# Attention with a feed-forward network on one core: the third step of pairs 2 and 3 computes block product 4 where the next pair's first FFN group stood, and the FFN groups move behind it

## The chip, the cores and the metric

The kernel runs on one core of one Trainium2 chip. The metric is the device time of one execution in microseconds. Ratios are worked out from the mean times of the fast runs of both kernels in the same rounds on the same chip, so they are not quite the ratio of the medians, nor always that of the plain means, that are quoted beside them. The span of a profiled execution is about 1.8 us shorter than its device time.

## The reference

Attention with a window of 96 keys and 8 global keys over 4 batches, 8 heads, 768 positions and a head size of 64. Its output, laid out as 3072 tokens of 512 values, goes through a feed-forward network (FFN) with a hidden size of 2048.

```python
scores = q @ k.T / sqrt(64) + bias         # kept: 8 global keys and the last 96 keys
a = softmax(where(keep, scores, -1e9))
x = (a @ v).transpose(0, 2, 1, 3).reshape(3072, 512)
r = maximum(x @ w_in, 0.0)                 # 512 -> 2048
out = (s * r * r + b) @ w_out              # 2048 -> 512
```

## The kernel before

The tokens are cut into 12 granules of 256. A step does the attention of two head pairs of one granule (two attention blocks, `stage_A`), computes the scores of the following step ahead of time, and has three slots, `c0`, `c1` and `c2`, for other work: the first goes before the first attention block, the second between the two blocks, the third after the second. A granule takes two steps.

In the second step of granule j its normalized attention output `xn` is transposed into `xT` by two DMA transposes in the SP queue. `u1(j, q)` is one FFN group of granule j: 16 matmuls that read `xT[j]` and `w_in` for a quarter of the hidden size, then a relu on ScalarE.

```python
    def finish_granule(j):
        ...
            x_by_dma(j)                      # xT[j] <- xn[j], two DMA transposes in the SP queue
        if 6 <= j + LEAD < NJ:
            hold_loads(xT[j][0:1, 0, GT - 1 : GT])   # loads of granule j+4 wait for xT[j]
            load_granule(j + LEAD)                   # six loads in the POOL queue: k, q, v, k, q, v

    def step(s, c0, c1, c2, pool=None, pre=()):
        ...
        if not last and j >= 4 and j + 2 < NJ:
            qk_by_dma(j + 2)                 # four DMA transposes in the SP queue
        posts = scores(s + 1)                # matmuls of the next step's scores
        ...
        run(exps); run(pre); run(masks)
        run(c0)
        stage_A(2 * s)                       # first attention block; normalized on VectorE
        flush()
        ...
        run(c1)
        stage_A(2 * s + 1, pool)             # second attention block, same PSUM buffer
        flush()
        ...
        run(c2[0:n])
        if last:
            finish_granule(j)
            if SHIFT < j + 2 < NJ:
                load_voff(j + 2)             # two more loads in the SP queue
        run(c2[n:])
        flush()
```

The second FFN matmul of two granules (a pair: granules 2*pr and 2*pr+1) is done as a 2x2 block product with seven block products in place of eight. `product(pr, n)` is one of them, 16 matmuls; `pe(pr, n)` is the product with its eviction queued for the next `flush`; `evac` reads its PSUM buffer on VectorE or ScalarE; `g_sum` and `weight_sums` make the sums of blocks that the products need, on VectorE; `join` adds partial results. Product 4 needs the last weight sum, `t4`. Products, FFN groups and some transposes share three PSUM buffers (`ps_h`); the attention blocks of these steps share one (`ps_av`).

Pairs 2, 3 and 4 run in this loop; pair pr starts at step 4*pr + 5. Its third step (`k0 + 2`, step 15 for pair 2) begins the FFN of granule 6, the next pair's first.

```python
    for pr in range(2, NJ // 2):
        ...
        step(
            k0 + 1,
            [u1(o, 2)],
            [u1(o, 3), g_sum(pr, 1, 0)],
            [g_sum(pr, 1, 1), pe(pr, 7), g_sum(pr, 2)],
            pre=[g_sum(pr, 3, 1)],
        )
        tail = k0 + 3 >= NU // 2
        step(
            k0 + 2,
            [u1(e + 2, 0), pe(pr, 5)] if tail else [pe(pr, 5), flush, pe(pr, 6)],
            [pe(pr, 6), g_sum(pr, 4, 0)] if tail else [g_sum(pr, 4, 0), u1(e + 2, 0)],
            [g_sum(pr, 4, 1), u1(e + 2, 1), join(pr, 1)] + [weight_sums[3]] * (pr == 2),
        )
        if tail:
            break
        step(
            k0 + 3,
            [pe(pr, 4)],
            [join(pr, 2), u1(e + 2, 2)],
            [u1(e + 2, 3)],
            pre=[join(pr, 0), pe(pr, 3), flush],
        )
```

The softmax here doesn't subtract the row's maximum and nothing guards it: scores larger than these inputs give would overflow.

Of the kernel before, what the change touches and what calls it, by code (L numbers as in the profile page):

```python
# [17 lines left out]
def kernel(  # L18
# [694 lines left out]
    def moe_p2_cols(j, tb, parts):  # L713
# [35 lines left out]
    weight_sums = [  # L749
        lambda: nc.vector.tensor_tensor(t1, w12, w11, ALU.subtract),  # L750
        lambda: nc.vector.tensor_tensor(t2, w22, t1, ALU.subtract),  # L751
        lambda: nc.vector.tensor_tensor(t3, w22, w12, ALU.subtract),
        lambda: nc.vector.tensor_tensor(t4, w21, t2, ALU.subtract),
    ]
# [3 lines left out]
    def quarter(j, half, c=None):  # L758
        lo, n = (0, NH) if c is None else (c * NH // 2, NH // 2)
        return g_of(j)[:, half * NH + lo : half * NH + lo + n, :]  # L760

    def g_sum(pr, n, c=None):

        def go():
            if pr not in gs_cur:
                gs_cur[pr] = [
                    gpool.tile([P, NH, GT], BF16, name="gsum", tag=f"gsum{i}", bufs=1)
                    for i in range(4)
                ]
            e, o = 2 * pr, 2 * pr + 1  # L770
            cs = slice(0, NH) if c is None else slice(c * NH // 2, (c + 1) * NH // 2)
            s1, s2, s3, s4 = (t[:, cs, :] for t in gs_cur[pr])
            dst, x, y, op = {
                1: (s1, quarter(o, 0, c), quarter(o, 1, c), ALU.add),
                2: (s2, s1, quarter(e, 0, c), ALU.subtract),
                3: (s3, quarter(e, 0, c), quarter(o, 0, c), ALU.subtract),
                4: (s4, quarter(e, 1, c), s2, ALU.subtract),
            }[n]
            nc.vector.tensor_tensor(dst, x, y, op)  # L779

        return go

    def unit_p1(j, q):

        for fp in (2 * q, 2 * q + 1):
            relu, _ = p1_mm(j, fp)
            relu()
        gs = g_of(j)[:, 4 * q : 4 * q + 4, :]
        if j % 2 or q == 3:
            outs.append(lambda: nc.vector.tensor_tensor(gs, gs, gs, ALU.mult))  # L790
        else:
            nc.scalar.activation(gs, gs, ACT.Square)
# [4 lines left out]
    def product(pr, n, tbs=range(GB), ps=None, cols=None):  # L797

        j = 2 * pr
        stat = {  # L800
            1: lambda: quarter(j, 0),
            2: lambda: quarter(j, 1),
            3: lambda: gs_cur[pr][3],
            4: lambda: quarter(j + 1, 1),
            5: lambda: gs_cur[pr][0],
            6: lambda: gs_cur[pr][1],
            7: lambda: gs_cur[pr][2],
        }[n]()
        mov = {1: w11, 2: w21, 3: w22, 4: t4, 5: t1, 6: t2, 7: t3}[n]
        cs = slice(0, CH) if cols is None else cols  # L810
        if ps is None:
            ps = ps_h.tile([P, GB, CH], F32, name="ps_2", tag="psh")
        prod_ps[pr, n] = ps
        for tb in tbs:
            for fc in range(NH):
                nc.tensor.matmul(  # L816
                    ps[:, tb, cs],
                    lhsT=stat[:, fc, tb * P : (tb + 1) * P],
                    rhs=mov[:, fc, cs],
                    start=(fc == 0),  # L820
                    stop=(fc == NH - 1),
                )

    def scaled(dst, ps, add):
        nc.vector.scalar_tensor_tensor(
            out=dst, in0=ps, scalar=s_bc[:], in1=add, op0=ALU.mult, op1=ALU.add
        )
# [6 lines left out]
    def both_blocks(ap):  # L834
        return ap.unsqueeze(1).to_broadcast((P, GB, CH))

    def put(pr, row, col, o, tb=None, c0=0, eng=nc.sync):

        b, g = divmod(2 * pr + row, NGR)
        t0 = b * S + g * GT  # L840
        cs = slice(col * CH, (col + 1) * CH)
        if tb is not None:
            t0 += tb * P
            c0 += col * CH
            eng.dma_start(out[t0 : t0 + P, c0 : c0 + o.shape[-1]], o)
        else:
            nc.sync.dma_start(out[t0 : t0 + GT, cs].rearrange("(a p) c -> p a c", p=P), o)
# [3 lines left out]
    def out_tile():  # L851

        n_out[0] += 1
        tag, bufs = (("first", 4), ("o_sb", 3))[n_out[0] % 2]
        return work.tile([P, GB, CH], F32, name="o_q", tag=tag, bufs=bufs)

    def store(pr, row, col, ps, add):

        o = out_tile()
        scaled(o[:].rearrange("p a c -> p (a c)"), ps, add)  # L860
        put(pr, row, col, o[:])

    def add_f32(dst, x, y):
        nc.vector.tensor_tensor(dst, x, y, ALU.add)

    def evac(pr, n):

        ps3 = prod_ps[pr, n][:]
        ps = ps3.rearrange("p a c -> p (a c)")
        if n == 1:  # L870
            res[pr] = [
                work.tile([P, GB, CH], F32, name=f"part{i}", tag=f"part{i}", bufs=1)
                for i in range(3)
            ]
            res[pr].append(out_tile() if pr == NJ // 2 - 1 else res[pr][0])
        r0, r1, r7, r6 = (t[:].rearrange("p a c -> p (a c)") for t in res[pr])
        if n == 1:
            scaled(res[pr][0][:], ps3, both_blocks(bvec[:, 0:CH]))
        elif n == 2:
            store(pr, 0, 0, ps, r0)  # L880
        elif n == 5:
            scaled(res[pr][1][:], ps3, both_blocks(bdiff[:]))
        elif n == 6:
            scaled(r6, ps, r0)
        elif n == 7:
            nc.scalar.activation(r7, ps, ACT.Copy, scale=s_bc[:])
        elif n == 3:
            store(pr, 0, 1, ps, r1)
        elif n == 4:
            store(pr, 1, 0, ps, r6)  # L890

    def join(pr, n):

        def go():
            _, r1, r7, r6 = (t[:].rearrange("p a c -> p (a c)") for t in res[pr])
            if n == 1:
                add_f32(r1, r1, r6)
            elif n == 0:
                add_f32(r6, r6, r7)
            else:  # L900
                o = out_tile()
                add_f32(o[:].rearrange("p a c -> p (a c)"), r7, r1)
                put(pr, 1, 1, o[:])

        return go

    def pe(pr, n):

        def go():
            product(pr, n)  # L910
            outs.append(lambda: evac(pr, n))

        return go

    def u1(j, q):
        return lambda: unit_p1(j, q)

# [214 lines left out]
    def rest(j, tb):  # L1132
# [6 lines left out]
    step(  # L1139
        11,  # L1140
        [lambda: p2_mm(3, 1, 0, FC // 2), u1(4, 0)],
        [u1(4, 1)],
        late[2:4] + [shifted_copy, weight_sums[0]],
    )
    step(12, [lambda: rest(3, 1), u1(4, 2)], [weight_sums[1], u1(4, 3)], [weight_sums[2]])
    for pr in range(2, NJ // 2):
        e, o = 2 * pr, 2 * pr + 1
        k0 = 2 * e + 5
        if k0 >= NU // 2:
            break  # L1150
        step(
            k0,
            [pe(pr, 2)],
            [u1(o, 0)],
            [u1(o, 1), flush, g_sum(pr, 3, 0)],
            pre=[pe(pr, 1), flush],
        )
        step(
            k0 + 1,
            [u1(o, 2)],  # L1160
            [u1(o, 3), g_sum(pr, 1, 0)],
            [g_sum(pr, 1, 1), pe(pr, 7), g_sum(pr, 2)],
            pre=[g_sum(pr, 3, 1)],
        )
        tail = k0 + 3 >= NU // 2
        step(
            k0 + 2,
            [u1(e + 2, 0), pe(pr, 5)] if tail else [pe(pr, 5), flush, pe(pr, 6)],
            [pe(pr, 6), g_sum(pr, 4, 0)] if tail else [g_sum(pr, 4, 0), u1(e + 2, 0)],
            [g_sum(pr, 4, 1), u1(e + 2, 1), join(pr, 1)] + [weight_sums[3]] * (pr == 2),  # L1170
        )
        if tail:
            break
        step(
            k0 + 3,
            [pe(pr, 4)],
            [join(pr, 2), u1(e + 2, 2)],
            [u1(e + 2, 3)],
            pre=[join(pr, 0), pe(pr, 3), flush],
        )  # L1180
    join(pr, 0)()
    for n in (3, 4):
# [4 lines left out]
    e, o = 2 * pr, 2 * pr + 1  # L1187
# [50 lines left out]
```

## Time and profile before

| | before |
|---|---|
| median of 3 runs | 210.3 us (210.06 to 210.32) |
| profiled execution | 210.51 us, span 208.7 us |
| PE busy | 201.1 us, 96% of the span |
| VectorE, ScalarE busy | 160.0 us (77%), 128.6 us (62%) |

The page of the kernel before, first the span and the busy time of each engine, then the granted clock in 40 slices (9 stands for nine tenths of full speed or more; the mean of this run was 1.000), then the shares of the chain that ended last:

```profile
span 208.7 us, 5315 instructions
...
PE 201.1 (96%) x2183; PEld 160.0 (77%) x2191; DVE 160.0 (77%) x336; ACT 128.6 (62%) x200; POOL 68.9 (33%) x89
...
PEclk9999999999999999999999999999999999999999
...
PE 76%; DMA 9%; POOL 4%; SPq 4%; DVE 3%; issue 1%; POOLq 0%
```

TensorE is the bound. The busy times of three stretches of the kernel before (columns: stretch in us and its length, then for each engine busy us and instructions, the clock, the DMA share and GB/s) show where it is not busy late in the kernel:

```profile
...
113.40:114.60 1.20, 0.07 (x3) 0.06 (x2) 1.09 (x3) 0.00 (x0) 0.04 (x1) 1.00 1.51 122
114.60:130.00 15.40, 15.40 (x176) 13.43 (x177) 10.50 (x20) 10.73 (x15) 8.51 (x12) 1.00 1.52 140
130.00:182.00 52.00, 51.98 (x597) 45.07 (x596) 40.28 (x79) 31.23 (x45) 2.31 (x3) 1.00 0.65 92
```

The PE timeline of the kernel before in step 15 (columns: start us, length us, engine, line, operation, out<-in, shape, count, and in brackets the idle time before it and what ended it). The lines left out are the attention matmuls:

```profile
109.41 3.78 PE L816 MATMUL ps<-wsub,gsum 128*128 128x256 bf16 x32
...
114.57 1.91 PE L616 MATMUL ps<-xT,w_in_bf 128*128 128x256 bf16 x16 [1.13 <-DMA xT<-xn]
...
116.56 1.91 PE L616 MATMUL ps<-xT,w_in_bf 128*128 128x256 bf16 x16
118.40 0.62 PE L438 MATMUL ps_s<-qx,kx 64*128 64x128 bf16 x16
118.95 1.92 PE L816 MATMUL ps<-w_out_bf,gsum 128*128 128x256 bf16 x16
```

Products 5 and 6 start at 109.41. The first FFN group of granule 6 waits 1.13 us for the transposed activations. Where nothing waits, the next matmuls start 1.75 us after the start of a group that is listed as 1.91 us long: the listed times overlap by 0.16 us. The page "Perfetto Trace Analysis" of the Trainium skill (summary of the profiler window per engine type) calls the TensorE end estimated, and this trace agrees in so far as the listed end is not when the next matmul can start.

The SP queue of the kernel before, which issued those transposes (the length is that of issuing, not of the transfer):

```profile
101.31 0.53 SPq L684 DMA_DIRECT2D out_dram<-o_sb  x1
101.94 0.44 SPq L847 DMA_DIRECT2D out_dram<-o_q  x1
102.54 3.46 SPq L596 DMA_TRANSPOSE xT<-xn  x2
106.12 0.93 SPq L313 DMA_DIRECT2D vo<-vb  x1
```

The last line of the view of line 596, all transposes of activations in the kernel before:

```profile
DMA to landing us min/median/max: 2.4/4.3/9.9
```

The maximum, 9.9 us, is the transpose of granule 6 (the same view cut to 101 to 108 us gives 9.9 alone). A load that waits for the same landing shows when it came; the POOL timeline of the kernel before:

```profile
114.56 0.18 POOL L122 COPY gate<-xT 1x1 bf16<-1x1 bf16 x1 [12.69 <-DMA xT<-xn]
```

VectorE in the same step of the kernel before. The lines are, in order: the sum for product 6, the masks of the next step, the eviction of product 5, the reciprocal and the normalizing of the first attention block, then the reciprocal of the second, and the weight sum t4 in its old place:

```profile
109.94 1.23 DVE L779 TENSOR_TENSOR gsum<-gsum,gT 128x2048 bf16<-128x2048 bf16 x1
111.08 1.28 DVE L454 TENSOR_TENSOR pt<-pt,tmpl 128x1024 bf16<-128x1024 bf16 x2
112.29 0.74 DVE L825 SCALAR_TENSOR_TENSOR part<-ps,s_bc,bdiff 128x512 f32<-128x512 f32 x1
113.48 0.18 DVE L462 RECIPROCAL rc<-ps_av 128x4 f32<-128x4 f32 x1 [0.45 <-PE ps_av L492]
113.69 0.42 DVE L463 TENSOR_TENSOR xn<-ps_av,rc 128x256 bf16<-128x256 f32 x1
...
116.75 0.18 DVE L462 RECIPROCAL rc<-ps_av 128x4 f32<-128x4 f32 x1 [1.38 <-PE ps_av L492]
...
118.52 1.22 DVE L753 TENSOR_TENSOR wsub<-w_out_bf,wsub 128x2048 bf16<-128x2048 bf16 x1
```

### The profile page before, as it was taken

What the parts mean: (1) busy time and instruction counts of PE and PEld (TensorE: products, weight loads), DVE (VectorE), ACT (ScalarE), POOL (GpSimd) and SP (SyncE); (2) the same over time, 40 slices, a digit from 0 to 9 for tenths busy, and PEclk for the clock granted to TensorE, in tenths of its full rate; (3) what the DMA queues carried; (4) which work ended last, traced back from release to release, by engine and by line L of the source; (5) the groups of instructions that cost most, each with busy time, mean ns of one, the idle gap of its engine ahead of it and who ended that gap; (6) DMA issues with size and microseconds to landing.
All of it is one profiled execution on the core that took longest, in us unless ns stands there. A gap on an engine that the chain in (4) does not pass through costs nothing.

```text
span 208.7 us, 5315 instructions
## 1 busy us (share of the span) xinstructions
PE 201.1 (96%) x2183; PEld 160.0 (77%) x2191; DVE 160.0 (77%) x336; ACT 128.6 (62%) x200; POOL 68.9 (33%) x89
## 2 busy tenths in 40 slices
PE   6899999999999999999997999999999999999993
PEld 2677884557867585878886898888898889888883
DVE  7685689995989866799799784599785696737974
ACT  4975669485975558685763766564966665476200
POOL 8984334999646102705500906300000000000000
PEclk9999999999999999999999999999999999999999
DMA  5999999999999999999999999999451210240006
GB/s 167 170 181 206 207 207 172 155 152 135 115 147 143 155 157 193 120 265 188 145 207 128 113 133 174 184 208 100 52 158 49 77 28 0 50 154 0 0 4 200
DMA packets 110308, 28.17 MB, mean 135 GB/s; under 512 B 97836, under 2 KB 108780, under 8 KB 110284
## 3 DMA queue, kind: packets, MB, share of 16 engines
q0 software_dynamic: 75472, 13.11, 86.7%
q1 hardware_dynamic: 33612, 14.13, 39.0%
q10 hardware_dynamic: 1200, 0.59, 1.1%
q8 instruction: 17, 0.28, 0.6%
q14 instruction: 7, 0.06, 0.1%
HBM read 27.26 MB, written 6.29 MB: 161 GB/s over the span
## 4 chain that ended last, share of the span: by engine, by line
PE 76%; DMA 9%; POOL 4%; SPq 4%; DVE 3%; issue 1%; POOLq 0%
PE ps L616 35%; PE ps L816 19%; PE ps L664 13%; DMA xT<-xn 5%; DMA w_in_bf<-in_moe_w_in_dram 5%; PE ps_s L438 4%; PE ps_av L492 4%; SPq L357 3%; POOL nat L102 2%; POOL vb L108 2%; SPq L596 1%; PE ps_t L348 1%; POOL w_in_bf L140 1%; DVE o_early L697 1%; DVE wsub L751 1%
## 5 line engine op out<-in xcount | busy, mean ns | idle before, releaser
L616 PE MATMUL ps<-xT,w_in_bf 128*128 128x256 bf16 x768 | 90.5, 273 | 1.7 <-DMA xT<-xn 1.1
L626 ACT ACTIVATE gT<-ps 128x512 bf16<-128x512 f32 x96 | 55.7, 598 | 48.4 <-PE ps L616 48.2
L616 PEld LDWEIGHTS <-w_in_bf 128*128 128x128 bf16 x768 | 72.8, 98 | 11.3 <-issue 1.2
L447 ACT ACTIVATE pt<-ps_s 128x1024 bf16<-128x1024 f32 (+1 forms) x44 | 39.3, 946 | 3.2 <-PE ps_s L438 3.2
L664 PE MATMUL ps<-w_out_bf,gT 128*128 128x512 bf16 x120 | 28.9, 379 | 0.5 <-issue 0.2
L816 PEld LDWEIGHTS <-gsum 128*128 128x128 bf16 x256 | 24.1, 98 | 3.7 <-DVE gsum L779 0.5
L454 DVE TENSOR_TENSOR pt<-pt,tmpl 128x1024 bf16<-128x1024 bf16 (+1 forms) x40 | 24.5, 644 | 1.7 <-ACT pt L447 1.6
L790 DVE TENSOR_TENSOR gT<-gT 128x1024 bf16<-128x1024 bf16 x20 | 13.7, 685 | 11.6 <-ACT gT L626 11.6
L664 PEld LDWEIGHTS <-gT 128*128 128x128 bf16 x128 | 11.7, 98 | 13.2 <-issue 0.3
L463 DVE TENSOR_TENSOR xn<-ps_av,rc 128x256 bf16<-128x256 f32 x48 | 20.4, 424 | 1.7
L116 POOL DMA_DIRECT2D nat<-in_k_dram x20 | 17.7, 886 | 8.6 <-DMA w_in_bf<-in_moe_w_in_dram 2.1
L816 PEld LDWEIGHTS <-gT 128*128 128x128 bf16 x200 | 18.7, 98 | 2.3
L117 POOL DMA_DIRECT2D vb<-in_v_dram x20 | 18.4, 919 | 5.9 <-DMA nat<-in_k_dram 2.4
L116 POOL DMA_DIRECT2D nat<-in_q_dram x20 | 17.9, 896 | 6.9 <-DMA w_out_bf<-in_moe_w_out_dram 2.9
L462 DVE RECIPROCAL rc<-ps_av 128x4 f32<-128x4 f32 x48 | 8.6, 178 | 12.8 <-PE ps_av L492 10.6
L492 PEld LDWEIGHTS <-pt 128*128 128x128 bf16 x320 | 14.4, 98 | 2.7 <-DVE xn L463 0.7
L629 DVE TENSOR_TENSOR gT<-gT 128x512 bf16<-128x512 bf16 x32 | 13.0, 420 | 3.7 <-ACT gT L626 3.3
L492 PE MATMUL ps_av<-vb,pt 128*128 128x65 bf16 x208 | 15.4, 193 | 0.0
L816 PE MATMUL ps<-w_out_bf,gsum 128*128 128x256 bf16 x128 | 15.3, 273 | 0.0
L816 PE MATMUL ps<-wsub,gsum 128*128 128x256 bf16 x128 | 15.1, 273 | 0.0
L122 POOL COPY gate<-xT 1x1 bf16<-1x1 bf16 x6 | 1.1, 190 | 40.6 <-DMA xT<-xn 39.5
L816 PE MATMUL ps<-w_out_bf,gT 128*128 128x256 bf16 x120 | 13.9, 273 | 0.0
(112 smaller groups left out, 221.8 us busy)
## 6 DMA issues: line engine op xcount, KB each, us to landing
out_dram<-o_q SPq DMA_DIRECT2D x15, 256.0 KB, 2.3
vb<-in_v_dram POOLq DMA_DIRECT2D x24, 128.0 KB, 7.4
nat<-in_k_dram POOLq DMA_DIRECT2D x22, 128.0 KB, 6.9
nat<-in_q_dram POOLq DMA_DIRECT2D x22, 128.0 KB, 7.3
w_out_bf<-in_moe_w_out_dram POOLq DMA_DIRECT2D x4, 512.0 KB, 17.2
w_in_bf<-in_moe_w_in_dram POOLq DMA_DIRECT2D x3, 512.0 KB, 11.2
out_dram<-o_sb SPq DMA_DIRECT2D x4, 256.0 KB, 6.1
out_dram<-o_early SPq DMA_DIRECT2D x4, 256.0 KB, 5.2
```

Source lines behind the costliest of these rows:

```text
L116: nc.gpsimd.dma_start(t[:, n, i, :, :], rows_of(srcs[n], b, sb))
L117: nc.gpsimd.dma_start(vbuf[b % 2][:, sb, :, 0:D], rows_of(v, b, sb))
L447: nc.scalar.activation(pt[:, :, 0:ncol], ps[:, :, 0:ncol], ACT.Exp, scale=QSCALE)
L454: nc.vector.tensor_tensor(pv, pv, m.rearrange("p h a c -> p h (a c)"), ALU.mult)
L463: nc.vector.tensor_tensor(dst, av[:, :, :, 0:D], rc[:].to_broadcast((P, 2, 2, D)), ALU.mult)
L492: nc.tensor.matmul(av[:, i, hi, 0 : D + 1], lhsT=pt[:, hi, c * P : (c + 1) * P], rhs=vv, start=(n == 0), stop=(n == len(terms) - 1),)
L616: nc.tensor.matmul(ps[:, i, :], lhsT=w_in_bf[:, kc, fc * P : (fc + 1) * P], rhs=xT[j][:, kc, :], start=(kc == 0), stop=(kc == KC - 1),)
L626: nc.scalar.activation(gs, ps[:], ACT.Relu)
L629: nc.vector.tensor_tensor(gs, gs, gs, ALU.mult)
L664: nc.tensor.matmul(po[:], lhsT=g_of(j)[:, fc, tb * P : (tb + 1) * P], rhs=w_out_bf[:, fc, :], start=(fc == 0), stop=(fc == FC - 1),)
L790: outs.append(lambda: nc.vector.tensor_tensor(gs, gs, gs, ALU.mult))
L816: nc.tensor.matmul(ps[:, tb, cs], lhsT=stat[:, fc, tb * P : (tb + 1) * P], rhs=mov[:, fc, cs], start=(fc == 0), stop=(fc == NH - 1),)
```

## The change

The intent is to give the transposes of the next pair's first granule more time. Product 4 needs nothing from them, so in pairs 2 and 3 (pair 4 keeps its order) it moves from the fourth step into the third, into the slot of the first of that granule's two FFN groups there; the first group moves behind the second attention block, and the second group into the fourth step, to product 4's old place. Product 4 needs the weight sum t4, which therefore moves into the second step. Its result is evicted in the fourth step.

```diff
+    def prod(pr, n):
+        return lambda: product(pr, n)
...
         step(
             k0 + 1,
             [u1(o, 2)],
             [u1(o, 3), g_sum(pr, 1, 0)],
-            [g_sum(pr, 1, 1), pe(pr, 7), g_sum(pr, 2)],
+            [g_sum(pr, 1, 1), pe(pr, 7), g_sum(pr, 2)] + [weight_sums[3]] * (pr == 2),
             pre=[g_sum(pr, 3, 1)],
         )
...
             k0 + 2,
             [u1(e + 2, 0), pe(pr, 5)] if tail else [pe(pr, 5), flush, pe(pr, 6)],
-            [pe(pr, 6), g_sum(pr, 4, 0)] if tail else [g_sum(pr, 4, 0), u1(e + 2, 0)],
-            [g_sum(pr, 4, 1), u1(e + 2, 1), join(pr, 1)] + [weight_sums[3]] * (pr == 2),
+            [pe(pr, 6), g_sum(pr, 4, 0)] if tail else [g_sum(pr, 4, 0), prod(pr, 4)],
+            [g_sum(pr, 4, 1), u1(e + 2, int(tail)), join(pr, 1)],
         )
...
             k0 + 3,
-            [pe(pr, 4)],
+            [u1(e + 2, 1)],
             [join(pr, 2), u1(e + 2, 2)],
             [u1(e + 2, 3)],
-            pre=[join(pr, 0), pe(pr, 3), flush],
+            pre=[join(pr, 0), lambda: evac(pr, 4), pe(pr, 3), flush],
         )
```

## The prediction

> **What bounds the kernel.** TensorE. PE is busy 201.1 of 208.7 us (96%), at full clock in every slice (the page); the chain of waits gives PE 76% of the span. From 114.6 us to 182 us PE is busy 67.4 of 67.4 us (busy time by stretch). The change adds and removes no instruction; it reorders a few in pairs 2 and 3. It can only win back PE idle time, or make new.
>
> **The idle there is.** In the PE timeline of the steps touched there is one hole: 113.43 to 114.57 us, 1.13 us, released by the DMA xT<-xn. It is the first matmul of the first FFN group of granule 6, third step of pair 2. The transpose of granule 6 was issued at 104.5 us and landed 9.9 us later (median of these transposes 4.3 us, this one the longest). Pair 3 has no hole there (145.2 us).
>
> **What the change does.** Block product 4 (16 matmuls 128x256, 1.75 us on PE) goes into that hole, and the FFN group comes one place later, behind the second attention block: 113.28 + 1.75 + 0.24 = 115.27 us at the earliest. The transpose lands at about 114.5, so 0.75 us to spare. PE gains 1.13 us if product 4 and its followers find all they need:
>
> - t4 (weight sum, VectorE, 1.22 us) moves a step earlier, behind the sum for product 6: about 111.1 to 112.3 us, needed at 113.28. Spare 1.0.
> - VectorE is then later by 1.13 us less the 0.45 us it idled before the next reciprocal. First attention block normalized at about 114.7; the single ps_av buffer is needed at 115.03. Spare 0.3, the tightest.
> - PSUM: the third step now holds product 4's result until the next step. The built program's order shows that product 3 does not take that buffer but the one of the first FFN half, freed by a relu at about 116.8, needed at 117.57. Product 4's own buffer comes free with its eviction, about 119.1, and is taken by an FFN half at about 120.2.
> - Second half of the sum for product 3: done at about 117.1, needed at 118.0.
>
> These are sums of start-to-start times in the timelines of VectorE, ScalarE and PE. I take VectorE and ScalarE as strict FIFO (Trainium skill, "TensorE: Matmul & The Clock Gate", architectural detail); their timelines show no reordering.
>
> Everything later comes 1.1 us earlier; the other transposes and loads have 3 us or more to spare (granule 7's lands at 126.4, needed at 129.6), so the gain should reach the end. Pair 3: same motion, same margins, change 0 within 0.1 us.
>
> **Predicted.** 210.3 - 1.1 = 209.2 us, range 208.8 to 209.8. Faster by over 2%: 0.01. Within 2%: 0.98. Slower by over 2%: 0.01.
>
> **What would show it.** The hole before the matmuls of granule 6's first group is gone, product 4 stands there with no wait, PE idle falls from 7.6 to about 6.5 us, PE busy stays 201 us. No new wait of over 0.2 us on product 4, the second attention block of the third step, or product 3.
>
> **What would make it wrong.** The transpose lands later than 115.3 us, so part of the wait stays; the first normalize comes later than I reckon and PE waits for ps_av; a transpose or load later in the kernel, not PE, was about to bind, and eats the 1.1 us; or the hole is shorter in timed runs than in the profiled one (210.51 us, above all three timed).

## The result, and the profile after

The changed kernel took 209.61 us (median of 4 runs, 209.53 to 209.70) against 210.31 us (4 runs, 210.06 to 210.74); the ratio is 0.9965, with a 95% interval of 0.9947 to 0.9982. That is 0.7 us, inside the predicted range and two thirds of the predicted 1.1 us.

The page of the changed kernel:

```profile
span 207.9 us, 5315 instructions
...
PE 201.8 (97%) x2183; PEld 160.4 (77%) x2191; DVE 160.9 (77%) x336; ACT 128.7 (62%) x200; POOL 69.5 (33%) x89
```

PE was idle for 207.9 - 201.8 = 6.1 us, against 7.6 us before. The PE timeline of the changed kernel in step 15:

```profile
109.93 3.78 PE L816 MATMUL ps<-wsub,gsum 128*128 128x256 bf16 x32
...
113.80 1.91 PE L816 MATMUL ps<-wsub,gT 128*128 128x256 bf16 x16
...
115.78 1.91 PE L616 MATMUL ps<-xT,w_in_bf 128*128 128x256 bf16 x16
117.62 0.62 PE L438 MATMUL ps_s<-qx,kx 64*128 64x128 bf16 x16
118.18 1.92 PE L816 MATMUL ps<-w_out_bf,gsum 128*128 128x256 bf16 x16
```

Product 4 stands at 113.80 and nothing in the step waits. A measure that does not depend on the listed ends is the distance from the start of products 5 and 6 to the start of product 3: it was 118.95 - 109.41 = 9.54 us and is now 118.18 - 109.93 = 8.25 us. So the step gave 9.54 - 8.25 = 1.29 us in this pair of traces. From there to the end of the span it is the same in both: 208.7 - 118.95 = 89.75 and 207.9 - 118.18 = 89.72 us, and in the twelve traces of the experiments it is 89.7 to 89.8 us, too. Nothing of the gain was lost later.

But the span fell by only 0.8 us. The rest is at the other end: products 5 and 6 started 0.52 us later in the changed kernel's trace (109.93 against 109.41), although both kernels have the same instructions up to there. The PE timeline of the changed kernel shows one cause, a wait for a weight load that the trace of before does not have:

```profile
34.81 4.48 PE L664 MATMUL ps<-w_out_bf,gT 128*128 128x512 bf16 x20 [0.31 <-DMA w_out_bf<-in_moe_w_out_dram]
```

The transposes of granule 6 landed at nearly the same time; the POOL timeline of the changed kernel:

```profile
114.81 0.18 POOL L122 COPY gate<-xT 1x1 bf16<-1x1 bf16 x1 [11.70 <-DMA xT<-xn]
```

VectorE in the changed kernel, the lines that answer to those of before (sum for product 6, t4 in its new place, masks, eviction of product 5, reciprocal and normalizing of the first attention block, and the eviction of product 4):

```profile
110.46 1.23 DVE L779 TENSOR_TENSOR gsum<-gsum,gT 128x2048 bf16<-128x2048 bf16 x1
111.61 1.22 DVE L753 TENSOR_TENSOR wsub<-w_out_bf,wsub 128x2048 bf16<-128x2048 bf16 x1
112.74 1.28 DVE L454 TENSOR_TENSOR pt<-pt,tmpl 128x1024 bf16<-128x1024 bf16 x2
113.95 0.74 DVE L825 SCALAR_TENSOR_TENSOR part<-ps,s_bc,bdiff 128x512 f32<-128x512 f32 x1
114.61 0.17 DVE L462 RECIPROCAL rc<-ps_av 128x4 f32<-128x4 f32 x1
114.81 0.42 DVE L463 TENSOR_TENSOR xn<-ps_av,rc 128x256 bf16<-128x256 f32 x1
...
119.00 0.75 DVE L825 SCALAR_TENSOR_TENSOR o_q<-ps,s_bc,part 128x512 f32<-128x512 f32 x1
```

t4 was ready at 112.83, 0.97 us before product 4 started, and the first attention block was normalized at 115.23, 0.3 us before the second one needed the buffer at 115.54.

Two readings of the missing 0.4 us were then open. Either the wait of before is not the same in every run (the profiled one, 210.51 us, had a long one), or it is, and the changed kernel gives something back. The experiments were made to tell these apart, to say which part of the change carries the gain, and to find what sets the length of the wait.

### The profile page after: what moved, and what is told of

Read it like the earlier page. It is cut to its first block, busy times and chain, and to the rows that moved or that the text cites. A ratio compares the mean times of both kernels' runs of the same rounds, so it can differ in the third digit from the quotient of the medians.

```text
span 207.9 us, 5315 instructions
## 1 busy us (share of the span) xinstructions
PE 201.8 (97%) x2183; PEld 160.4 (77%) x2191; DVE 160.9 (77%) x336; ACT 128.7 (62%) x200; POOL 69.5 (33%) x89
## 4 chain that ended last, share of the span: by engine, by line
PE 79%; DMA 13%; POOL 4%; DVE 3%; issue 1%; POOLq 0%
PE ps L616 34%; PE ps L816 24%; PE ps L664 10%; DMA w_out_bf<-in_moe_w_out_dram 9%; PE ps_s L438 4%; PE ps_av L492 4%; DMA w_in_bf<-in_moe_w_in_dram 3%; POOL nat L102 2%; POOL vb L108 1%; PE ps_t L348 1%; DVE wsum L642 1%; DVE pt L454 1%; PE ps_last L816 0%; PE ps_x L588 0%; DVE vo L394 0%
## 5 line engine op out<-in xcount | busy, mean ns | idle before, releaser
L117 POOL DMA_DIRECT2D vb<-in_v_dram x20 | 17.9, 895 | 6.4 <-DMA nat<-in_k_dram 2.9
L122 POOL COPY gate<-xT 1x1 bf16<-1x1 bf16 x6 | 2.1, 349 | 39.3 <-DMA xT<-xn 37.1
```

The source lines that it names most:

```text
L117: nc.gpsimd.dma_start(vbuf[b % 2][:, sb, :, 0:D], rows_of(v, b, sb))
```

## The experiments

Twelve runs were made (e1 and e8 of unchanged kernels), each with five timed rounds beside the kernel before. "Step time" below is the distance from the start of products 5 and 6 to the start of product 3, in the one profiled execution of each kernel. 8.25 us is the step without a wait, so the step time less 8.25 us is the wait. The medians are of six executions, the profiled one and the five timed ones.

| run | what it is | median us (range) | ratio to before (95%) | step time, wait in us |
|---|---|---|---|---|
| before (first profile) | | 210.3 (210.06 to 210.32) | | 9.54, 1.29 |
| changed | | 209.61 (209.53 to 209.70) | 0.9965 (0.9947 to 0.9982) | 8.25, 0 |
| e1_before_again | before | 209.90 (209.57 to 210.90) | 1.0001 (0.9972 to 1.0029) | 8.56, 0.31 |
| e2_pair2_only | change in pair 2 only | 209.47 (209.21 to 209.79) | 0.9973 (0.9948 to 0.9997) | 8.25, 0 |
| e3_pair3_only | change in pair 3 only | 209.96 (209.36 to 211.06) | 0.9998 (0.9966 to 1.003) | 8.37, 0.12 |
| e4_sum_only | t4 moved only | 209.86 (209.37 to 211.13) | 1.0001 (0.9967 to 1.0035) | 8.51, 0.26 |
| e5_before_late_xT | before, transposes issued later | 209.80 (209.21 to 209.93) | 0.9969 (0.9949 to 0.9989) | 8.59, 0.34 |
| e6_after_late_xT | changed, transposes issued later | 209.64 (209.52 to 209.97) | 0.9969 (0.995 to 0.9988) | 8.25, 0 |
| e7_after_late_sum | changed, t4 just before product 4 | 210.55 (210.11 to 210.68) | 1.0002 (0.998 to 1.0023) | 9.20, 0.95 |
| e8_after_again | changed | 209.61 (209.31 to 209.86) | 0.9965 (0.9945 to 0.9984) | 8.24, 0 |
| e9_before_loads_early | before, four loads moved away | 210.85 (210.53 to 211.72) | 1.0038 (1.0014 to 1.0061) | 8.25, 0 |
| e10_before_stores_late | before, two stores behind the transposes | 209.51 (209.24 to 209.73) | 0.9969 (0.9949 to 0.999) | 8.25, 0 |
| e11_after_v_last | changed, v loaded last | 209.24 (209.10 to 209.57) | 0.9959 (0.9937 to 0.9981) | 8.25, 0 |
| e12_after_v_last_again | the same again | 209.54 (209.48 to 209.83) | 0.9974 (0.9943 to 1.0004) | 8.24, 0 |

Each row compares with the runs of before on its own chip and occasion (e1 to e4 together: 210.16 us median, 209.14 to 211.27; e5 to e8: 210.35, 209.44 to 211.00; e9 to e11: 210.16, 209.54 to 210.85; e12: 210.26, 209.31 to 211.28).

### e1: the kernel before as its own control

> The kernel before, unchanged, as its own control. Hole theory: the gain of the change is the wait of PE for the transposed activations of granule 6, and the wait is the landing less PE's arrival at that place; PE's arrival hangs on the opening (its start was 0.52 us later in the changed kernel's trace), so the wait differs from run to run and is below 1.13 us in most: here between 0.5 and 1.2 us. Rival, later loss: the wait is 1.13 us every time, and the changed kernel gives 0.4 us back after it. Ratio 1.000 within 0.002.

No edit. The PE timeline of this run:

```profile
109.82 3.78 PE L816 MATMUL ps<-wsub,gsum 128*128 128x256 bf16 x32
114.00 1.91 PE L616 MATMUL ps<-xT,w_in_bf 128*128 128x256 bf16 x16 [0.15 <-DMA xT<-xn]
```

The same kernel has a wait of 0.31 us here (bracket 0.15) where its first profile had 1.29 us (bracket 1.13). PE arrived 0.41 us later and the landing came 0.57 us earlier (114.00 against 114.57), so both ends of the wait move from run to run. The first theory put it down mostly to PE's arrival; the trace shows both. The measured wait is below the 0.5 to 1.2 us that was expected. The timed runs spread from 209.57 to 210.90 us.

### e2, e3, e4: the parts of the change

> The change in pair 2 alone (with the weight sum moved), pair 3 as before. Hole theory: all of the gain, ratio 0.9965 within 0.0015, no wait before granule 6's first group. Rival, that the order is better in each pair: about half the gain, 0.998.

> The change in pair 3 alone, pair 2 and the weight sum as before. Hole theory: nothing, 1.000 within 0.001, and pair 2 keeps its wait of 0.5 to 1.2 us. Rival, that the order is better in each pair: about half the gain, 0.998.

> Only the last weight sum moved a step earlier on VectorE; the products stay. Hole theory: nothing, 1.000 within 0.001; the wait stays, VectorE's idle time before the second attention block's reciprocal (1.38 us) takes the 1.2 us up. Rival, that the sum on VectorE was in the way of the next step: part of the gain, 0.998 or less.

The edits (e2 and e3 have the new order behind a test on the pair, shown here against the changed kernel; e3 also keeps the weight sum where before has it):

```diff
# e2: P = 2; e3: P = 3
-            [...] if tail else [g_sum(pr, 4, 0), prod(pr, 4)],
-            [g_sum(pr, 4, 1), u1(e + 2, int(tail)), join(pr, 1)],
+            [...] if tail else [g_sum(pr, 4, 0), prod(pr, 4) if pr == P else u1(e + 2, 0)],
+            [g_sum(pr, 4, 1), u1(e + 2, 0 if pr == P else 1), join(pr, 1)],
...
-            [u1(e + 2, 1)],
+            [u1(e + 2, 1)] if pr == P else [pe(pr, 4)],
...
-            pre=[join(pr, 0), lambda: evac(pr, 4), pe(pr, 3), flush],
+            pre=[join(pr, 0)] + ([lambda: evac(pr, 4)] if pr == P else []) + [pe(pr, 3), flush],
# e4: the kernel before, with
-            [g_sum(pr, 1, 1), pe(pr, 7), g_sum(pr, 2)],
+            [g_sum(pr, 1, 1), pe(pr, 7), g_sum(pr, 2)] + [weight_sums[3]] * (pr == 2),
...
-            [g_sum(pr, 4, 1), u1(e + 2, 1), join(pr, 1)] + [weight_sums[3]] * (pr == 2),
+            [g_sum(pr, 4, 1), u1(e + 2, 1), join(pr, 1)],
```

Pair 2 alone gave 0.9973, pair 3 alone 0.9998, the moved sum alone 1.0001. Pair 2 carries the gain, within what these intervals resolve; neither pair 3 nor the place of the sum gives anything that can be seen. The waits that e3 and e4 keep were 0.12 and 0.26 us in their profiled executions (209.37 us both, at the low end of their runs), below the 0.5 us that was expected. Each of them also had one long execution, 211.06 and 211.13 us; none of e2, e6, e8, e10, e11 and e12, whose traces have no wait in this step, had one above 209.97 us. The mean of the four profiled waits with the transposes issued as before (first profile, e1, e3, e4) is (1.29 + 0.31 + 0.12 + 0.26) / 4 = 0.50 us. Four samples are few, and the last two are of short executions, so the mean of all runs is likely above 0.50 us; but they leave no room for 1.1 us in every run.

### e5, e6: the transposes issued later

> The kernel before, with granule 6's transposes put behind two loads of the same queue (they took 2.3 us there), so that they land some 2 us later. Hole theory: the wait before granule 6's first group grows by about that, to 2 to 3.3 us; time up by 1.5 to 2.5 us, ratio 1.007 to 1.012. Rival, that the wait is no part of the time that counts (other waits would end it anyway): ratio within 0.002 of 1.

> The same delay in the changed kernel. Hole theory: the group comes 2.0 us later there (product 4 1.75 us and an attention block 0.24 us), so the delay is hidden but for what goes over: a wait of 0 to 1.3 us, and the difference to the delayed kernel before is 1.7 to 2.0 us, about three times the gain without the delay. Rival, that the gain has another cause than the transposes: the difference stays at the 0.6 to 0.75 us seen.

```diff
         if last:
+            if j == 6:
+                load_voff(j + 2)
             finish_granule(j)
-            if SHIFT < j + 2 < NJ:
+            if SHIFT < j + 2 < NJ and j != 6:
                 load_voff(j + 2)
```

This was a miss, and it was the useful one. The SP queue of e5, then its PE timeline:

```profile
105.09 3.35 SPq L596 DMA_TRANSPOSE xT<-xn  x2
```

```profile
114.02 1.91 PE L616 MATMUL ps<-xT,w_in_bf 128*128 128x256 bf16 x16 [0.18 <-DMA xT<-xn]
```

The transposes were issued at 105.09 in place of 102.78 (e1), 2.3 us later, and PE could start at 114.02 in place of 114.00. The landing did not move with the issue at all. So e5 added no delay and could not be the test of the hidden 2 us that it was meant to be; e6 has nothing to hide either, and both came out at 0.9969: the difference between them is zero, which neither reading of e6 expected. Why e5 is faster than before in the timed runs, where its one profile still shows a wait of 0.34 us, is open; its spread (209.21 to 209.93) suggests that its long waits are rarer. The other traces say the same. In before, the changed kernel, e1 to e4, e7 and e8 the transposes were issued at 102.54 to 103.56 and the load held for them went at 112.04 (e2) to 115.08 us (e7); in e5 and e6, issued at 105.09 and 106.11, it went at 114.01 and 113.55. What follows is that, within this spread of issues, the landing is set by something other than the time of issue, and e9 and e10 look for it.

### e7: the price of a wait in this place

> The changed kernel, but the weight sum (1.22 us on VectorE) just before product 4 instead of at the end of the step before. Margin theory: t4 is then ready at about 114.7 us of the trace's time where product 4 could start at 113.8, so PE waits 0.6 to 1.0 us there and the gain is lost: 0.6 to 1.0 us over the changed kernel, ratio to before 1.000 to 1.003. Rival, that VectorE has slack enough anywhere in this step: equal to the changed kernel, 0.997.

```diff
-            [g_sum(pr, 1, 1), pe(pr, 7), g_sum(pr, 2)] + [weight_sums[3]] * (pr == 2),
+            [g_sum(pr, 1, 1), pe(pr, 7), g_sum(pr, 2)],
...
-            [...] if tail else [pe(pr, 5), flush, pe(pr, 6)],
+            [...] if tail else [pe(pr, 5), flush, pe(pr, 6)] + [weight_sums[3]] * (pr == 2),
```

The VectorE timeline of e7 at the weight sum, then its PE timeline:

```profile
113.45 1.22 DVE L753 TENSOR_TENSOR wsub<-w_out_bf,wsub 128x2048 bf16<-128x2048 bf16 x1
```

```profile
114.72 1.92 PE L816 MATMUL ps<-wsub,gT 128*128 128x256 bf16 x16 [0.78 <-DVE wsub L753]
```

t4 was ready at 114.67 and product 4 started at 114.72. The step took 9.20 us, 0.95 us more than without a wait, and the kernel lost about the same: 210.44 us on the mean against 209.61 us of the changed kernel in the same rounds, 0.83 us. So a wait here costs about what it lasts, in the time that counts, and the earlier place of t4 gives nothing by itself (e4) but is needed for the gain.

### e8: the changed kernel again

> The changed kernel unchanged, beside these. 0.997 within 0.0015; spread of its runs half that of before or less, since the wait that varied is gone; no wait of PE between 90 and 180 us.

No edit. 0.9965 again, 209.31 to 209.86 us, where the eleven runs of before beside it went from 209.44 to 211.00 us. The lower end is nearly the same; it is the upper end that the change takes away. The standard deviation of the runs is 0.22 us against 0.49 us. The trace has no wait for the transposes; one opening wait that differs from trace to trace is in its PE timeline:

```profile
60.69 0.34 PE L438 MATMUL ps_s<-qx,kx 64*128 64x128 bf16 x6 [0.48 <-DMA qx<-nat]
```

### e9, e10: what makes the transposes land when they do

> The kernel before, but four of the six loads of granule 9, which ran beside granule 6's transposes, are issued some 10 us earlier, behind those of granule 8. Traffic theory: the transposes landed at 113.3 to 114.4 us in five traces of kernels with that traffic, issued at 102.5 or at 105.1 alike, because the transfers drain together; with four loads fewer they land by about 110, and the wait (0 to 1.3 us) is gone with the order of before: ratio 0.997, narrow spread. A cost may come instead at granule 5's transposes, which now share the engines (they landed 2.5 us before they were needed). Rival, the transposes themselves are slow or wait for stores in their own queue: landing still at 113 to 114, ratio 1.000.

> The kernel before, but the two output stores that stood just before granule 6's transposes in their queue are put behind them. Queue theory: the transposes are issued about 1.2 us earlier and land 2 us or more earlier, no wait, ratio 0.997. Rival, load traffic alone decides: landing still at 113 to 114, wait 0.1 to 1.3 us, ratio 0.999 to 1.000.

```diff
# e9: in finish_granule of the kernel before
-            load_granule(j + LEAD)
+            if j == 5:
+                load_v(j + LEAD)
+            else:
+                load_granule(j + LEAD)
+            if j == 4:
+                for i in range(GB):
+                    load_qk(9, i)
# e10: the kernel before; the stores of granule 3's second half and of pair 2's
# product 2 are collected in `held` where they were issued, and
             finish_granule(j)
+            if j == 6:
+                run(held)
```

In e9 the wait before granule 6's group is gone (step time 8.25 us). The load held for the transposes went at 112.54 us, against 113.42 to 114.56 us in the four traces with the old traffic and order, so it would probably have been gone, too, had PE not come 1.4 us later. But the same load went at 112.04 us in e2, where no load was moved, so the earlier landing of granule 6 in the one trace of e9 is within what varies anyway. And the kernel is slower by 0.8 us on the mean. The loads were put beside the transposes of granule 5, which landed 8.6 us after their issue in place of 4.5 us (4.2 to 5.9 us in all the other traces), and PE waited there instead. The last line of the view of line 596 of e9 cut to 83 to 96 us, where granule 5's transposes were issued, then its PE timeline:

```profile
DMA to landing us min/median/max: 8.6/8.6/8.6
```

```profile
100.34 1.92 PE L616 MATMUL ps<-xT,w_in_bf 128*128 128x256 bf16 x16 [1.41 <-DMA xT<-xn]
```

In the kernel before that group started at 98.48 with no wait. The wait followed the loads from one granule's transposes to the other's. This is what the page "DMA: Bandwidth & Descriptors" of the Trainium skill says (issuing engines are not separate DMA queues): DMAs run on the same 16 engines and interleave, whichever engine started them. The loads are issued by POOL and the transposes by SP, and loads of the one slowed transposes of the other, 8.6 against 4.5 us.

In e10 the order of before, with two stores behind the transposes, was as fast as the changed kernel: 0.9969. The SP queue of e10, then its PE timeline:

```profile
101.92 2.69 SPq L596 DMA_TRANSPOSE xT<-xn  x2
```

```profile
109.77 3.78 PE L820 MATMUL ps<-wsub,gsum 128*128 128x256 bf16 x32
113.64 1.91 PE L616 MATMUL ps<-xT,w_in_bf 128*128 128x256 bf16 x16
```

The transposes were issued 0.9 us earlier than in e1, and the load held for them went at 111.69 us in place of 113.99, 2 us before PE needed them. The group followed products 5 and 6 with no wait, 3.87 us after their start, which is the distance at which product 4 follows them in the changed kernel. Why e10 lands earlier is not shown by its one trace: 111.69 is only a little below the 112.04 us of e2, which moved no store; it is the narrow timed runs (209.24 to 209.73 us) that say that the wait is gone. The traces hold one more witness, read from the DMA packets of the POOL queue. In the ten traces with the same loads (before, the changed kernel, e1 to e8) the last packet of the six loads of granule 9 started between 107.91 (e2) and 112.32 us (e8), and the transposes landed 2.0 to 5.2 us after it. Landing and last packet go together (correlation 0.83); landing and issue do not (-0.19). That speaks for the traffic theory, but it is a correlation, and together with e5 and e10 the cause of the landing time stays partly open. e10 also shows that the order of the products is not itself worth anything: with the wait gone by another way, the old order is as fast as the new one, as far as intervals of 0.002 either way resolve it.

### e11, e12: an attempt at a better kernel

> An attempt at a better kernel: the changed kernel with each granule's loads in the order k, q, k, q, v, v instead of k, q, v, k, q, v. Aimed at the wait for granule 4's transposed queries at 60.7 us (0.25 to 0.48 us in three of the traces so far): the second block's queries are loaded 0.9 us earlier. If that wait is what is left to win: about 0.2 us over the changed kernel, 0.9955 to before. If not: the same as the changed kernel, 0.997; a late v block would show as a wait of the second matmul.

> The changed kernel with the v blocks loaded last once more, on another occasion, because the last step of 0.06% (0.9959 against 0.9965 of the changed kernel beside another set of runs of before) is smaller than the intervals. If it is real: 0.9955 to 0.9963, no wait for granule 4's queries at 60 us in the trace. If it was the luck of one occasion: 0.9965 to 0.997.

```diff
             for n in range(2):
                 nc.gpsimd.dma_start(t[:, n, i, :, :], rows_of(srcs[n], b, sb))
-            nc.gpsimd.dma_start(vbuf[b % 2][:, sb, :, 0:D], rows_of(v, b, sb))
+        load_v(j)
```

The first occasion gave 0.9959, the second 0.9974, on both sides of the changed kernel's 0.9965. The wait for granule 4's queries was in neither trace, but other opening waits differ from run to run just as much. No version better than the changed kernel was found; what these runs show is that a step of 0.06% cannot be claimed from one occasion of six runs.

## Why the prediction was right, and what it mis-sized

- **What bounds the kernel: right.** PE was busy for all of the 12 us from 109 to 121 us in the changed kernel's trace, against 10.87 us before, at the same instruction count.
- **Where the gain lies: right.** It is the wait for granule 6's transposes in pair 2. Pair 2 alone gave 0.9973, pair 3 alone 0.9998.
- **No new wait: right.** The spare times were as reckoned: 0.97 us for t4 (reckoned 1.0), 0.3 us for the attention buffer (reckoned 0.3); the eviction of product 4 ended at 119.75, which is 0.13 us after the 119.1 of the prediction plus the 0.52 us by which the trace is later. VectorE and ScalarE ran in the order that the program gives, as the prediction took from the Trainium skill ("TensorE: Matmul & The Clock Gate", architectural detail). The moved sum was rightly named among the things that product 4 needs: put 1.84 us later (e7), past its spare of 0.97 us, it cost all of the gain.
- **The gain reaches the end: right.** 89.75 and 89.72 us from product 3 to the end, and 89.7 to 89.8 us in every other trace.
- **The size: two errors that partly cancel.** "PE gains 1.13 us" was read from the bracket of one trace. In that pair of traces the step gave 1.29 us, because the listed end from which the bracket counts is 0.16 us late. But the term that was mis-sized is the wait itself: it was taken as fixed, and it is the difference of two times that move from run to run, the landing and PE's arrival. Four profiled executions had 1.29, 0.31, 0.12 and 0.26 us. The profiled one of before was, at 210.51 us, slower than all three timed runs, and the prediction said so in its last sentence, as a thing that could make it wrong, without correcting for it. Three occasions of the timed runs give a mean gain of 0.75 us (changed), 0.57 us (e2, pair 2 alone) and 0.66 us (e8). The range, which allowed for a gain of 0.5 us, took this in; the central figure of 1.1 us rested on one long sample.
- **A rival for part of the missing gain stays open.** In the five traces with the new order in pair 2 and the old loads (changed, e2, e6, e7, e8) products 5 and 6 started at 109.91 to 110.20 us, in the six with the old order there (before, e1, e3, e4, e5, e10) at 109.32 to 109.82, although the product and the groups that were moved come later; e11 and e12 (new order, other loads) had 109.46 and 109.79. No run shows whether this is chance. The timed runs speak against a loss of that size: the old order without its wait (e10) took 209.50 us on the mean, the new order 209.50 (e2), 209.70 (e6) and 209.61 us (e8).
- **PE idle 7.6 to about 6.5 us, PE busy at 201 us: only partly.** It was 6.1 us idle and 201.8 us busy. The whole-kernel sums also hold the opening, which differs between traces (products 5 and 6 began between 109.32 and 110.20 us in the eleven traces of kernels with the same opening), so they are a poor witness for a 1 us step; the step time is the better one.
- **Risk named first, a transpose that lands later than the group: not met** in the traces of the changed kernel. The load held for the transposes went at 114.81 (first profile) and 114.59 (e8); the group needed them at 115.78 and 115.92. The spare was 0.97 and 1.33 us. In e12, with the v blocks last, it was 0.64 us (115.00 and 115.64).

## What to carry to other kernels

A wait for a DMA on the bounding engine is a difference of two moving times: one trace shows one sample of it, so profile the same kernel two or three times before putting a figure to its removal, and look at the spread of the timed runs, which shrinks when such a wait goes. Moving independent work ahead of the consumer, taking other transfers off the queue ahead of the transfer, or moving traffic away from it can all remove the same wait; what is gone cannot be won twice (e6, which has both the late issue and the new order, is no faster than either alone). Traffic that is moved lands on another transfer, so check that one's spare time first (e9 lost 0.8 us by it).

## What the Trainium skill lacked or had wrong

- "DMA: Bandwidth & Descriptors" (DMA transpose; latency and other measured facts) gives a rate for DMA transposes and latencies of single accesses, one of them under high load, but not how long a transpose takes to land beside other traffic: here the transposes of activations took 2.4 to 9.9 us, median 4.3, and in one place 6.6 to 9.9 us in different executions of equal transfers.
- The same page gives no figure for how far the landing of a transpose can part from its issue: issued at 102.78 or 105.09 us, PE could start on it at 114.00 or 114.02 us (e1, e5). The traces show that the landing goes with the end of the loads (correlation 0.83 over ten traces); no run here shows why.
- "Perfetto Trace Analysis" (summary of the profiler window per engine type) rightly calls the TensorE end estimated but gives no size: groups that follow each other with no wait start 1.75 us apart and are listed as 1.91 us long, so the wait in the bracket was 0.16 us short (1.13 against 1.29 us).
